# An mLSTM cell and a multiplicative feed-forward block in one kernel: output gate and weight exponential moved to ScalarE, units taken chunk by chunk, weight conversion spread over 18 units

## Chip, cores, metric

One NeuronCore of one Trainium2 chip. The metric is the device time of one execution in microseconds (us); medians of several runs. A run more than 1.5% above the fastest of its kernel counts as slow and is left out of the ratios. Engines in the profile: PE is TensorE (PEld its weight loads), DVE is VectorE, ACT is ScalarE, POOL is GpSimd, SP issues the transfers.

## The reference, cut to what matters

```python
# mLSTM cell: batch 4, heads 8, sequence 768, head dim 40; all float32
m_new  = max(f + m, i);  f_stab = exp(f + m - m_new);  i_stab = exp(i - m_new)
C = f_stab * C + i_stab * outer(v, k);   n = f_stab * n + i_stab * k
y = sigmoid(o) * (C @ q) / max(|n . q|, 1)
# then, on x = y as 3072 tokens x 320:
out = ((x @ w1) * (x @ w2)) @ w3 @ w_out     # d_ff 1024; the weights come as float64
```

## The kernel before

A **unit** is one chunk of 128 tokens of one batch with its 8 heads: 24 units. The loop has a **step** per unit. Its work on PE is: transposes of k and q (pt), scores (ss), state times q (pi), scores times v (ph), state update (pc), transposes of y (px). Four units make one group of 512 tokens for the feed-forward part: eight **ups** (128 columns of d_ff each: pa, pb) and four **downs** (128 tokens each: po). Before the downs, w3 and w_out have to be multiplied together, in eight **folds** (w3p, wp). The weights arrive as 64-bit words and are turned into float32 by seven DVE instructions per tile (34 **conversions**: 10 for w1 and w2, 8 for w_out, 16 for w3). In the views, pw is the tile of the weights that multiply the scores, h the cell's sum before the gate, y the result after it, st (later state) the state.

```python
def weights(n):                                     # b, c = divmod(n, NT): all chunks of a batch in turn
    nc.vector.tensor_tensor(out=pw, in0=pw, in1=aT[...], op=OP.add)              # pw [128, 8, 128]
    nc.gpsimd.affine_select(out=pw, in_=pw, ..., fill=-1.0e4, ...)
    nc.scalar.activation(out=pw, in_=pw, func=AF.Exp)
    nc.gpsimd.tensor_scalar(out=o, in0=o, scalar1=-87.0, scalar2=None, op0=OP.max)   # o [128, 320]
    nc.scalar.activation(out=o, in_=o, func=AF.Exp, scale=-1.0)
    nc.vector.tensor_scalar(out=o, in0=o, scalar1=1.0, scalar2=None, op0=OP.add)
    nc.vector.reciprocal(out=o, in_=o)
# ...
fold = {4: (0, 1), 5: (2,), 6: (3,), 7: (4, 5), 8: (6,), 9: (7,)}
for s in range(NU + LAG + 2 * GT):
    # ... loads for unit s + 2; weights(s); turn(s) (transposes)
    for _ in range(4):
        if w12_jobs:
            to_f32(*w12_jobs.pop(0))                # w1, w2: steps 0 to 2
    if 2 <= s < 4:
        for ko in range((s - 2) * FO // 2, (s - 1) * FO // 2):
            cvt_wo(ko)                              # w_out: steps 2, 3
    # ... first up; scores(s)
    for ko in fold.get(s, ()):
        cvt_w3(ko); w3_trans(ko); w3_mm(ko)         # w3: steps 4 to 9
    # ... cell(s - 1); second up; x_trans(s - 2); one down
```

## Time and profile before

| | before |
|---|---|
| median of 4 runs | 625.94 us (624.04 to 628.0) |
| span of the profiled run | 622.8 us |
| PE busy / DVE busy | 532.7 / 344.3 us |
| PE not busy | 622.8 - 532.7 = 90.1 us |

The prediction below shows the main views. One view is added here: what PE waited for in the first 300 us (engine, tile and line, released by; us in total, number of waits, the longest).

```profile
PE px L338 <- DVE h L289: 24.6, 2, 16.2
PE ss L273 <- DVE pw L276: 15.5, 2, 11.5
...
PE pi L287 <- DVE st L315: 11.8, 1, 11.8
PE wp L237 <- DVE w3T L231: 10.4, 5, 3.6
```

### The profile page before, as it was taken

How to read it: one execution, taken by the hardware profiler on the slowest of the kernel's cores; microseconds unless marked ns; L12 is line 12 of the kernel's file. 1: busy time of each engine (PE TensorE's matmuls, PEld its weight loads, DVE VectorE, ACT ScalarE, POOL GpSimd, SP SyncE). 2: the span in 40 equal slices, each digit the busy share in tenths (PEclk: the TensorE clock that was granted, in tenths of full speed). 3: DMA queues.
4: the chain of work that ended last, by engine and by line, in shares of the span. 5: the costliest groups of instructions: out<-in, count | busy, mean ns of one | idle time of the engine just before them, and what ended most of it. 6: DMA issues, size and time to landing. Idle time of an engine off the chain costs nothing.

```text
span 622.8 us, 6767 instructions
## 1 busy us (share of the span) xinstructions
PE 532.7 (86%) x2522; PEld 342.7 (55%) x2522; DVE 344.3 (55%) x648; ACT 118.9 (19%) x212; POOL 115.1 (18%) x129
## 2 busy tenths in 40 slices
PE   1362454588979899999999999999999999999997
PEld 1252353366646556665566665666665665554455
DVE  7499897988999844654464544644552332100000
ACT  2220011122122220222220222212221111111110
POOL 2261423323121121221121112211211000000000
PEclk9755555598999898999999999999999999999999
DMA  8698536446363132323334225334220000000001
GB/s 122 137 258 233 138 85 181 111 107 156 103 177 89 21 77 51 81 52 78 77 68 85 63 47 97 66 76 87 41 58 12 1 11 12 11 11 13 19 12 42
DMA packets 135488, 49.28 MB, mean 79 GB/s; under 512 B 103360, under 2 KB 131008, under 8 KB 135456
## 3 DMA queue, kind: packets, MB, share of 16 engines
q1 hardware_dynamic: 135456, 48.85, 33.8%
q8 instruction: 20, 0.33, 0.2%
q14 instruction: 12, 0.10, 0.1%
HBM read 44.81 MB, written 4.03 MB: 78 GB/s over the span
## 4 chain that ended last, share of the span: by engine, by line
PE 72%; DVE 17%; DMA 4%; SPq 2%; issue 2%; POOL 1%; ACT 0%; DVEq 0%; POOLq 0%; ACTq 0%
PE po L362 17%; PE pa L351 12%; PE pb L351 12%; PE pa L354 7%; PE wp L237 7%; PE ph L292 6%; PE pc L303 3%; PE pi L287 2%; PE ss L273 2%; PE pt L262 2%; DMA raw<-in_moe_w_dram 2%; DVE ex L138 2%; DVE mf L140 2%; DMA raw<-in_moe_w_out_dram 1%; SPq L107 1%
## 5 line engine op out<-in xcount | busy, mean ns | idle before, releaser
L357 DVE TENSOR_TENSOR ab<-pb,a_sb 128x512 f32<-128x512 f32 x48 | 33.0, 687 | 146.8 <-ACT a_sb L356 146.4
L362 PE MATMUL po<-w3o,ab 128*128 128x320 f32 x384 | 107.1, 434 | 0.0
L351 PE MATMUL pa<-xT,w 128*128 128x512 f32 x192 | 91.7, 600 | 0.0
L351 PE MATMUL pb<-xT,w 128*128 128x512 f32 x192 | 90.2, 592 | 0.0
L362 PEld LDWEIGHTS po<-w3o,ab 128*128 128x128 f32 x384 | 71.4, 190 | 30.3 <-issue 3.0
L356 ACT COPY a_sb<-pa 128x512 f32<-128x512 f32 x48 | 28.1, 584 | 237.6 <-PE pb L354 237.4
L351 PEld LDWEIGHTS pb<-xT,w 128*128 128x128 f32 x192 | 36.5, 190 | 45.9 <-issue 45.0
L246 DVE TENSOR_TENSOR pw<-pw,aT 128x1024 f32<-128x1024 f32 x24 | 29.8, 1242 | 45.1 <-DMA pw<-U_d 45.0
L292 PE MATMUL ph<-vbuf,pw 128*128 128x41 f32 x384 | 51.9, 298 | 3.1 <-ACT w3T L229 3.1
L354 PE MATMUL pa<-xT,wr 64*128 64x512 f32 x96 | 53.9, 641 | 0.0
L354 PE MATMUL pb<-xT,wr 64*128 64x512 f32 x96 | 53.9, 641 | 0.0
L292 PEld LDWEIGHTS ph<-vbuf,pw 128*128 128x128 f32 x384 | 50.7, 211 | 4.5 <-ACT w3T L229 3.4
L256 DVE RECIPROCAL o_in<-o_in 128x320 f32<-128x320 f32 x24 | 51.5, 2147 | 0.5
L237 PE MATMUL wp<-wo,w3T 128*128 128x320 f32 x128 | 42.8, 491 | 10.4 <-DVE w3T L231 10.4
L299 POOL TENSOR_TENSOR vw<-vbuf,wT 128x328 f32<-128x328 f32 x20 | 25.1, 1256 | 139.3 <-PE pc L303 123.4
L351 PEld LDWEIGHTS pa<-xT,w 128*128 128x128 f32 x192 | 33.2, 190 | 27.7 <-issue 26.7
L253 POOL TENSOR_SCALAR o_in<-o_in 128x320 f32<-128x320 f32 x24 | 36.5, 1519 | 60.9 <-DMA o_in<-in_o_gate_dram 60.9
L273 PE MATMUL ss<-qT,kT 64*128 64x128 f32 x384 | 31.8, 303 | 16.2 <-DVE pw L276 15.5
L273 PEld LDWEIGHTS ss<-qT,kT 64*128 64x128 f32 x384 | 30.2, 213 | 26.4 <-issue 13.2
L237 PEld LDWEIGHTS wp<-wo,w3T 128*128 128x128 f32 x128 | 26.7, 216 | 22.1 <-DVE w3T L231 11.6
L248 POOL TENSOR_SCALAR_AFFINE_SELECT pw<-pw 128x1024 f32<-128x1024 f32 x24 | 28.2, 1178 | 41.4 <-DVE pw L246 41.4
L338 PE MATMUL px<-ident,y 128*128 128x128 f32 x72 | 13.7, 302 | 24.6 <-DVE h L289 24.6
(77 smaller groups left out, 593.2 us busy)
## 6 DMA issues: line engine op xcount, KB each, us to landing
pw<-U_d SPq DMA_DIRECT2D x24, 512.0 KB, 5.3
raw<-in_moe_w_dram SPq DMA_DIRECT2D x24, 512.0 KB, 4.8
qbuf<-in_q_dram SPq DMA_DIRECT2D x24, 160.0 KB, 3.0
kbuf<-in_k_dram SPq DMA_DIRECT2D x24, 160.0 KB, 3.6
vbuf<-in_v_dram SPq DMA_DIRECT2D x24, 160.0 KB, 2.8
o_in<-in_o_gate_dram SPq DMA_DIRECT2D x24, 160.0 KB, 3.6
out_dram<-o_sb SPq DMA_DIRECT2D x24, 160.0 KB, 1.8
raw<-in_moe_w_out_dram SPq DMA_DIRECT2D x8, 320.0 KB, 3.3
```

Of the source, the lines that this page charges most:

```text
L237: nc.tensor.matmul(wp, lhsT=w3T[:, ki, :], rhs=wo[:, ki, :], start=(ki == 0), stop=(ki == FO - 1))
L246: nc.vector.tensor_tensor(out=pw, in0=pw, in1=aT[:, c, b * H:(b + 1) * H].unsqueeze(2).to_broadcast([L, H, L]), op=OP.add)
L248: nc.gpsimd.affine_select(out=pw, in_=pw, compare_op=OP.is_ge, fill=-1.0e4, base=0, pattern=[[0, H], [1, L]], channel_multiplier=-1)
L253: nc.gpsimd.tensor_scalar(out=o, in0=o, scalar1=-87.0, scalar2=None, op0=OP.max)
L256: nc.vector.reciprocal(out=o, in_=o)
L273: nc.tensor.matmul(ss[hip][:, p, :], lhsT=kT[r, p, :], rhs=qT[r, p, :], start=True, stop=True)
L292: nc.tensor.matmul(ph[:, hd, :], lhsT=pw[:, hd, :], rhs=vt[:, hd, :], start=True, stop=True)
L351: nc.tensor.matmul(p, lhsT=wt[:, cc, fs], rhs=x[:, cc, :], start=(cc == 0), stop=False)
L354: nc.tensor.matmul(p, lhsT=wr[r, fs], rhs=x[r, KF, :], start=False, stop=True)
L356: nc.scalar.copy(out=a_sb, in_=pa)
L357: nc.vector.tensor_tensor(out=ab_t[gr][:, f, :], in0=pb, in1=a_sb, op=OP.mult)
L362: nc.tensor.matmul(po, lhsT=ab_t[gr][:, f, j * L:(j + 1) * L], rhs=w3o[:, f, :], start=(f == 0), stop=(f == FO - 1))
```

## The change

Its intent: take work off DVE (the output gate becomes one Sigmoid on ScalarE for four units at once; the sum with `a` becomes the bias of the exponential), take the units chunk by chunk so that the state of a batch is needed only four units later, and hand out the conversions one to three a step, so that DVE's load fits beside the cell. A first stage for chunk 0 alone lets unit 0 start early.

```diff
-        nc.vector.tensor_tensor(out=pw, in0=pw, in1=aT[...], op=OP.add)
-        nc.gpsimd.affine_select(..., fill=-1.0e4, ...)
-        nc.scalar.activation(out=pw, in_=pw, func=AF.Exp)
+        for h in range(H):
+            nc.scalar.activation(out=pw[:, h, :], in_=pw[:, h, :], func=AF.Exp, bias=aT[:, c, b * H + h:...])
+        nc.gpsimd.affine_select(..., fill=0.0, ...)
-        # gate: max on GpSimd, exp on ScalarE, add and reciprocal on DVE, for each unit
+    def out_gate(c):
+        nc.scalar.activation(out=o_t[c], in_=o_t[c], func=AF.Sigmoid)      # [128, 4, 8, 40]
-        b, c = divmod(n, NT)
+        c, b = divmod(n, B)
-            st = sb.tile(...)                       # a new state tile for each unit
+        st = state[b]                               # one a batch, updated in place
-        nc.vector.tensor_scalar(out=den, in0=h[:, :, D:D1], scalar1=-1.0, scalar2=1.0, op0=OP.mult, op1=OP.max)
-        nc.vector.tensor_tensor(out=den, in0=h[:, :, D:D1], in1=den, op=OP.max)
+        nc.vector.tensor_scalar(out=den.bitcast(U32), ..., scalar1=0x7FFFFFFF, op0=OP.bitwise_and)
+        nc.vector.tensor_scalar(out=den, in0=den, scalar1=1.0, scalar2=None, op0=OP.max)
-    w1, w2: four a step from step 0; w_out: steps 2, 3; w3: steps 4 to 9
+    n_up = [0] * 6 + [2] * 8 + [0] * 6 + [2] * 6 + [4] * 5 + [0]
+    n_down = [0] * 18 + [2, 2, 1, 1, 1, 1, 2, 2, 0, 2, 2, 2, 2, 4]
+    cvt = {s: [("w12", 0, s)] for s in range(5)}
+    cvt.update({5: [w12 x3], 6: [w12 x2], 7: [wo x3], 8: [wo x3], 9: [wo x2]})          # shortened here
+    cvt.update({10 + ko: [("w3", ko)] for ko in range(8)})
```

Cut: the first stage for chunk 0, buffer counts (raw 3 to 2, xT 2 to 4), the mantissa of a conversion written in place.

More of the change, by code (lines that the diff above doesn't have):

```diff
@@ L54 @@
     REM = DM - KF * L
-    GT = 4
+    GT = B
     TG = GT * L
@@ L59 @@
     const = ctx.enter_context(tc.tile_pool(name="const", bufs=1))
-    gates = ctx.enter_context(tc.tile_pool(name="gates", bufs=1))
     wst = ctx.enter_context(tc.tile_pool(name="wst", bufs=2))
@@ L63 @@
     sb = ctx.enter_context(tc.tile_pool(name="sb", bufs=2))
-    ffn = ctx.enter_context(tc.tile_pool(name="ffn", bufs=2))
     dram = ctx.enter_context(tc.tile_pool(name="dram", bufs=1, space=bass.MemoryType.DRAM))
@@ L74, in mps @@
         return ps_m.tile(shape, FP, name=name, tag="m")
-    f_sb = gates.tile([BH, S], FP, name="f_sb")
-    a = gates.tile([BH, S], FP, name="a")
-    nc.sync.dma_start(out=f_sb, in_=f_gate.rearrange("b h s -> (b h) s"))
-    nc.sync.dma_start(out=a, in_=i_gate.rearrange("b h s -> (b h) s"))
     NB, NBQ = 4, 3
@@ L85 @@
     vbuf = [const.tile([L, H, D1], FP, name=f"vbuf{i}") for i in range(NB)]
-    for t in qbuf:
-        nc.gpsimd.memset(t[:, :, D:DP], 0.0)
-    for i in range(NB):
-        nc.gpsimd.memset(kbuf[i][:, :, D:DP], 0.0)
-        nc.gpsimd.memset(vbuf[i][:, :, D:D1], 1.0)
-    ident = const.tile([128, 128], FP, name="ident")
-    make_identity(nc, ident)
+    ident = const.tile([128, 128], FP, name="ident")
+    one = const.tile([BH, 1], FP, name="one")
+    state = [const.tile([128, NP, 2, D1], FP, name=f"state{b}") for b in range(B)]
@@ L95 @@
+    aT = const.tile([L, NT, BH], FP, name="aT")
+    gT = const.tile([L, NT, BH], FP, name="gT")
+    wT = const.tile([L, NT, BH], FP, name="wT")
+    decP = const.tile([128, B * NP, NT], FP, name="decP")
+    U_d = [dram.tile([BH, L], FP, name=f"U_d{c}") for c in range(NT)]
+    dec_d = dram.tile([BH, NT], FP, name="dec_d")
     o_t, u_t = {}, {}
     def load(n):
-        b, c = divmod(n, NT)
-        o_t[n] = io.tile([L, H, D], FP, name="o_in", tag="o_in", bufs=4)
-        for dst, src in ((qbuf[n % NBQ][:, :, 0:D], q), (kbuf[n % NB][:, :, 0:D], k),
-                         (vbuf[n % NB][:, :, 0:D], v), (o_t[n][:], o_gate)):
+        c, b = divmod(n, B)
+        for dst, src in ((qbuf[n % NBQ][:, :, 0:D], q), (kbuf[n % NB][:, :, 0:D], k), (vbuf[n % NB][:, :, 0:D], v)):
@@ L102, in load, with load_o @@
             nc.sync.dma_start(out=dst, in_=src[b, :, c * L:(c + 1) * L, :].rearrange("h p d -> p h d"))
+    def load_o(c):
+        o_t[c] = io.tile([L, B, H, D], FP, name="o_in", tag="o_in", bufs=2)
+        for b in range(B):
+            nc.sync.dma_start(out=o_t[c][:, b], in_=o_gate[b, :, c * L:(c + 1) * L, :].rearrange("h p d -> p h d"))
     def load_u(n):
-        b, c = divmod(n, NT)
+        c, b = divmod(n, B)
         u_t[n] = io.tile([L, H, L], FP, name="pw", tag="pw", bufs=4)
-        nc.sync.dma_start(out=u_t[n], in_=U_d[b * H:(b + 1) * H, c * L:(c + 1) * L]
-                          .unsqueeze(0).to_broadcast([L, H, L]))
@@ L110, with gate_cols @@
-    load(0)
-    load(1)
+        nc.sync.dma_start(out=u_t[n], in_=U_d[c][b * H:(b + 1) * H, :].unsqueeze(0).to_broadcast([L, H, L]))
+    with tc.tile_pool(name="gates", bufs=1) as gates:
+        f_sb = gates.tile([BH, S], FP, name="f_sb")
+        a = gates.tile([BH, S], FP, name="a")
+        nc.sync.dma_start(out=f_sb, in_=f_gate.rearrange("b h s -> (b h) s"))
+        nc.sync.dma_start(out=a, in_=i_gate.rearrange("b h s -> (b h) s"))
+        load(0)
+        nc.vector.memset(one, 1.0)
+        make_identity(nc, ident)
+        for i in range(NB):
+            nc.gpsimd.memset(kbuf[i][:, :, D:DP], 0.0)
+            if i < NBQ:
+                nc.gpsimd.memset(qbuf[i][:, :, D:DP], 0.0)
+            nc.gpsimd.memset(vbuf[i][:, :, D:D1], 1.0)
+        for t in state:
+            nc.gpsimd.memset(t, 0.0)
+        F = gates.tile([BH, S], FP, name="F")
+        U = gates.tile([BH, S], FP, name="U")
+        g, w = F, f_sb
+        m0 = gates.tile([BH, NT], FP, name="m0")
+        dec = gates.tile([BH, NT], FP, name="dec")
+        def gate_cols(src, dst, c0, c1):
+            pg = tps([L, c1 - c0, BH], "pg")
+            for c in range(c0, c1):
+                nc.tensor.transpose(pg[:, c - c0, :], src[:, c * L:(c + 1) * L], ident[0:BH, 0:BH])
+            nc.vector.tensor_copy(out=dst[:, c0:c1, :], in_=pg)
+        nc.vector.tensor_copy(out=f_sb[:, 0:1], in_=a[:, 0:1])
+        for c0, c1 in ((0, 1), (1, NT)):
+            rs = slice(c0 * L, c1 * L)
+            for c in range(c0, c1):
+                r = slice(c * L, (c + 1) * L)
+                nc.vector.tensor_tensor_scan(out=F[:, r], data0=one.to_broadcast([BH, L]), data1=f_sb[:, r], initial=0.0,
+                                             op0=OP.mult, op1=OP.add)
+                if c > 0:
+                    nc.vector.tensor_scalar(out=a[:, r], in0=a[:, r], scalar1=m0[:, c:c + 1], scalar2=None,
+                                            op0=OP.subtract)
+                nc.vector.tensor_tensor_scan(out=U[:, r], data0=f_sb[:, r], data1=a[:, r],
+                                             initial=0.0 if c else -1.0e30, op0=OP.add, op1=OP.max)
+                if c == 0:
+                    nc.vector.tensor_copy(out=m0[:, 1:2], in_=U[:, L - 1:L])
+                elif c < NT - 1:
+                    nc.vector.tensor_tensor(out=m0[:, c + 1:c + 2], in0=m0[:, c:c + 1],
+                                            in1=U[:, (c + 1) * L - 1:(c + 1) * L], op=OP.add)
+            nc.vector.tensor_tensor(out=U[:, rs], in0=F[:, rs], in1=U[:, rs], op=OP.subtract)
+            for c in range(c0, c1):
+                nc.sync.dma_start(out=U_d[c], in_=U[:, c * L:(c + 1) * L])
+            nc.vector.tensor_tensor(out=a[:, rs], in0=a[:, rs], in1=F[:, rs], op=OP.subtract)
+            gate_cols(a, aT, c0, c1)
+            if c0 == 0:
+                for n in range(2):
+                    load_u(n)
+                load_o(0)
+                load(1)
+            U3, w3d, a3 = (x.rearrange("p (c t) -> p c t", t=L)[:, c0:c1] for x in (U, w, a))
+            nc.vector.tensor_tensor(out=w3d, in0=a3, in1=U3[:, :, L - 1:L].to_broadcast([BH, c1 - c0, L]), op=OP.add)
+            nc.scalar.activation(out=dec[:, c0:c1], in_=U3[:, :, L - 1], func=AF.Exp)
+            nc.scalar.activation(out=g[:, rs], in_=U[:, rs], func=AF.Exp)
+            nc.scalar.activation(out=w[:, rs], in_=w[:, rs], func=AF.Exp)
+            gate_cols(w, wT, c0, c1)
+            if c0 > 0:
+                gate_cols(g, gT, c0, c1)
+        nc.sync.dma_start(out=dec_d, in_=dec)
+        for hip in range(2):
+            nc.sync.dma_start(out=decP[hip * DP:(hip + 1) * DP],
+                              in_=dec_d.rearrange("(n two) c -> two n c", two=2)[hip:hip + 1]
+                              .to_broadcast([DP, B * NP, NT]))
@@ L114 @@
+    ffn = ctx.enter_context(tc.tile_pool(name="ffn", bufs=2))
     wo = const.tile([128, FO, DM], FP, name="wo")
@@ L126, in to_f32 @@
         n = dst.shape[-1]
-        raw = wst.tile([128, n, 2], U32, name="raw", tag="raw", bufs=3)
+        raw = wst.tile([128, n, 2], U32, name="raw", tag="raw", bufs=2)
         for rows, src in pieces:
@@ L132, in to_f32 @@
         ma = wst.tile([128, n], U32, name="ma", tag="ma")
-        mf = wst.tile([128, n], FP, name="mf", tag="mf")
+        mf = ma.bitcast(FP)
         V = nc.vector
@@ L146, with cvt_w12 @@
     every = slice(0, 128)
-    w12_jobs = []
-    for c0 in range(0, DFF, CW):
-        for dst, src in ((w1, w1_d), (w2, w2_d)):
-            for ko in range(KF):
-                w12_jobs.append((dst[:, ko, c0:c0 + CW], [(every, src[ko * 128:(ko + 1) * 128, cols(c0, CW)])]))
-        w12_jobs.append((wr[:, c0:c0 + CW], [(slice(j * REM, (j + 1) * REM), src[KF * L:DM, cols(c0, CW)])
-                                             for j, src in enumerate((w1_d, w2_d))]))
+    def cvt_w12(half, i):
+        c0 = half * CW
+        if i < 2 * KF:
+            dst, src = ((w1, w1_d), (w2, w2_d))[i // KF]
+            ko = i % KF
+            to_f32(dst[:, ko, c0:c0 + CW], [(every, src[ko * 128:(ko + 1) * 128, cols(c0, CW)])])
+        else:
+            to_f32(wr[:, c0:c0 + CW], [(slice(j * REM, (j + 1) * REM), src[KF * L:DM, cols(c0, CW)])
+                                       for j, src in enumerate((w1_d, w2_d))])
     def cvt_wo(ko):
@@ L161, in cvt_w3 @@
             to_f32(w3_t[ko][:, c0:c0 + CW], [(every, w3_d[ko * 128:(ko + 1) * 128, cols(c0, CW)])])
-    one = const.tile([BH, 1], FP, name="one")
-    nc.vector.memset(one, 1.0)
-    F = gates.tile([BH, S], FP, name="F")
-    U = gates.tile([BH, S], FP, name="U")
-    g, w = F, f_sb
-    m0 = gates.tile([BH, NT], FP, name="m0")
-    dec = gates.tile([BH, NT], FP, name="dec")
-    nc.vector.tensor_copy(out=f_sb[:, 0:1], in_=a[:, 0:1])
-    for c in range(NT):
-        r = slice(c * L, (c + 1) * L)
-        nc.vector.tensor_tensor_scan(out=F[:, r], data0=one.to_broadcast([BH, L]), data1=f_sb[:, r], initial=0.0,
-                                     op0=OP.mult, op1=OP.add)
-        if c > 0:
-            nc.vector.tensor_scalar(out=a[:, r], in0=a[:, r], scalar1=m0[:, c:c + 1], scalar2=None, op0=OP.subtract)
-        nc.vector.tensor_tensor_scan(out=U[:, r], data0=f_sb[:, r], data1=a[:, r], initial=0.0 if c else -1.0e30,
-                                     op0=OP.add, op1=OP.max)
-        if c == 0:
-            nc.vector.tensor_copy(out=m0[:, 1:2], in_=U[:, L - 1:L])
-        elif c < NT - 1:
-            nc.vector.tensor_tensor(out=m0[:, c + 1:c + 2], in0=m0[:, c:c + 1], in1=U[:, (c + 1) * L - 1:(c + 1) * L],
-                                    op=OP.add)
@@ L187 @@
-    nc.vector.tensor_tensor(out=U, in0=F, in1=U, op=OP.subtract)
-    U_d = dram.tile([BH, S], FP, name="U_d")
-    nc.sync.dma_start(out=U_d, in_=U)
-    nc.vector.tensor_tensor(out=a, in0=a, in1=F, op=OP.subtract)
-    U3 = U.rearrange("p (c t) -> p c t", t=L)
-    nc.vector.tensor_tensor(out=w.rearrange("p (c t) -> p c t", t=L), in0=a.rearrange("p (c t) -> p c t", t=L),
-                            in1=U3[:, :, L - 1:L].to_broadcast([BH, NT, L]), op=OP.add)
-    nc.scalar.activation(out=dec, in_=U3[:, :, L - 1], func=AF.Exp)
@@ L195 @@
-    nc.scalar.activation(out=g, in_=U, func=AF.Exp)
-    nc.scalar.activation(out=w, in_=w, func=AF.Exp)
-    aT = const.tile([L, NT, BH], FP, name="aT")
-    gT = const.tile([L, NT, BH], FP, name="gT")
-    wT = const.tile([L, NT, BH], FP, name="wT")
-    decP = const.tile([128, B * NP, NT], FP, name="decP")
-    dec_d = dram.tile([BH, NT], FP, name="dec_d")
-    nc.sync.dma_start(out=dec_d, in_=dec)
-    for hip in range(2):
-        nc.sync.dma_start(out=decP[hip * DP:(hip + 1) * DP],
-                          in_=dec_d.rearrange("(n two) c -> two n c", two=2)[hip:hip + 1]
-                          .to_broadcast([DP, B * NP, NT]))
@@ L210, in gate_cols @@
-    def gate_cols(src, dst):
-        pg = tps([L, NT, BH], "pg")
-        for c in range(NT):
-            nc.tensor.transpose(pg[:, c, :], src[:, c * L:(c + 1) * L], ident[0:BH, 0:BH])
-        nc.vector.tensor_copy(out=dst, in_=pg)
     w3T_t = {}
@@ L238, in w3_mm @@
         nc.scalar.copy(out=w3o[:, ko, :], in_=wp)
-    qT_t, kT_t, c_t, y_t, x_t, s_t, e_t = {}, {}, {}, {}, {}, {}, {}
+    qT_t, kT_t, y_t, x_t = {}, {}, {}, {}
+    def out_gate(c):
+        nc.scalar.activation(out=o_t[c], in_=o_t[c], func=AF.Sigmoid)
     def weights(n):
-        b, c = divmod(n, NT)
+        c, b = divmod(n, B)
         pw = u_t[n]
-        nc.vector.tensor_tensor(out=pw, in0=pw, in1=aT[:, c, b * H:(b + 1) * H].unsqueeze(2).to_broadcast([L, H, L]),
-                                op=OP.add)
-        nc.gpsimd.affine_select(out=pw, in_=pw, compare_op=OP.is_ge, fill=-1.0e4, base=0,
+        for h in range(H):
+            nc.scalar.activation(out=pw[:, h, :], in_=pw[:, h, :], func=AF.Exp, bias=aT[:, c, b * H + h:b * H + h + 1])
+        nc.gpsimd.affine_select(out=pw, in_=pw, compare_op=OP.is_ge, fill=0.0, base=0,
                                 pattern=[[0, H], [1, L]], channel_multiplier=-1)
-        nc.scalar.activation(out=pw, in_=pw, func=AF.Exp)
-        o = e_t[n] = o_t.pop(n)
-        nc.gpsimd.tensor_scalar(out=o, in0=o, scalar1=-87.0, scalar2=None, op0=OP.max)
-        nc.scalar.activation(out=o, in_=o, func=AF.Exp, scale=-1.0)
-        nc.vector.tensor_scalar(out=o, in0=o, scalar1=1.0, scalar2=None, op0=OP.add)
-        nc.vector.reciprocal(out=o, in_=o)
     def turn(n):
@@ L278, in cell @@
     def cell(n):
-        b, c = divmod(n, NT)
+        c, b = divmod(n, B)
         pw, vt = u_t.pop(n), vbuf[n % NB]
         qT = qT_t.pop(n)
+        st = state[b]
         hs = slice(b * H, (b + 1) * H)
@@ L287, in cell @@
                 nc.tensor.matmul(pi[:, 2 * p:2 * p + 2, :].rearrange("p a b -> p (a b)"), lhsT=qT[:, p, :],
-                                 rhs=c_t[n - 1][:, p].rearrange("p a b -> p (a b)"), start=True, stop=True)
+                                 rhs=st[:, p].rearrange("p a b -> p (a b)"), start=True, stop=True)
             nc.vector.tensor_tensor(out=h, in0=pi, in1=gT[:, c, hs].unsqueeze(2).to_broadcast([L, H, D1]), op=OP.mult)
@@ L305, in cell @@
                                  rhs=vw[:, 2 * p:2 * p + 2, :].rearrange("p a b -> p (a b)"), start=True, stop=True)
-            st = sb.tile([128, NP, 2, D1], FP, name="st", tag="st")
-            if c == 0:
-                nc.gpsimd.memset(st, 0.0)
-            else:
+            if c > 0:
                 nc.gpsimd.tensor_tensor(
-                    out=st.rearrange("p n a b -> p n (a b)"), in0=c_t[n - 1].rearrange("p n a b -> p n (a b)"),
+                    out=st.rearrange("p n a b -> p n (a b)"), in0=st.rearrange("p n a b -> p n (a b)"),
                     in1=decP[:, b * NP:(b + 1) * NP, c:c + 1].to_broadcast([128, NP, 2 * D1]), op=OP.mult)
@@ L315, in cell @@
                 nc.vector.tensor_tensor(out=st[r, :, hip, :], in0=pc[r, :, hip, :], in1=st[r, :, hip, :], op=OP.add)
-            c_t[n] = st
-        c_t.pop(n - 1, None)
         den = sb.tile([L, H, 1], FP, name="den", tag="den")
-        nc.vector.tensor_scalar(out=den, in0=h[:, :, D:D1], scalar1=-1.0, scalar2=1.0, op0=OP.mult, op1=OP.max)
-        nc.vector.tensor_tensor(out=den, in0=h[:, :, D:D1], in1=den, op=OP.max)
+        nc.vector.tensor_scalar(out=den.bitcast(U32), in0=h[:, :, D:D1].bitcast(U32), scalar1=0x7FFFFFFF, scalar2=None,
+                                op0=OP.bitwise_and)
+        nc.vector.tensor_scalar(out=den, in0=den, scalar1=1.0, scalar2=None, op0=OP.max)
         nc.vector.reciprocal(out=den, in_=den)
-        e = e_t.pop(n)
+        e = o_t[c][:, b]
         nc.vector.tensor_tensor(out=e, in0=e, in1=den.to_broadcast([L, H, D]), op=OP.mult)
@@ L333, in x_trans @@
         if j == 0:
-            x_t[gr] = ffn.tile([128, KF + 1, TG], FP, name="xT", tag="xT")
+            x_t[gr] = ffn.tile([128, KF + 1, TG], FP, name="xT", tag="xT", bufs=4)
         y = y_t.pop(n)
@@ L365, in ffn_out @@
         nc.scalar.copy(out=o_sb, in_=po)
-        t0 = (gr * GT + j) * L
+        t0 = j * S + gr * L
         nc.sync.dma_start(out=out[t0:t0 + L, :], in_=o_sb)
-    for n in range(3):
-        load_u(n)
-    gate_cols(a, aT)
-    gate_cols(g, gT)
-    gate_cols(w, wT)
-    LAG = 2
-    UPS = FO // GT
-    up = [(gr, f) for gr in range(NG) for f in range(FO)]
-    down = [(gr, j) for gr in range(NG) for j in range(GT)]
-    fold = {4: (0, 1), 5: (2,), 6: (3,), 7: (4, 5), 8: (6,), 9: (7,)}
-    for s in range(NU + LAG + 2 * GT):
-        u = s - LAG - GT
-        ups = up[u * UPS:(u + 1) * UPS] if u >= 0 else []
-        downs = down[u - GT:u - GT + 1] if u >= GT else []
+    LAG = 2
+    ups = [(gr, f) for gr in range(NG) for f in range(FO)]
+    downs = [(gr, j) for gr in range(NG) for j in range(GT)]
+    n_up = [0] * 6 + [2] * 8 + [0] * 6 + [2] * 6 + [4] * 5 + [0]
+    n_down = [0] * 18 + [2, 2, 1, 1, 1, 1, 2, 2, 0, 2, 2, 2, 2, 4]
+    cvt = {s: [("w12", 0, s)] for s in range(5)}
+    cvt.update({5: [("w12", 1, 0), ("w12", 1, 1), ("w12", 1, 2)], 6: [("w12", 1, 3), ("w12", 1, 4)]})
+    cvt.update({7: [("wo", i) for i in range(3)], 8: [("wo", i) for i in range(3, 6)], 9: [("wo", i) for i in range(6, 8)]})
+    cvt.update({10 + ko: [("w3", ko)] for ko in range(8)})
+    out_gate(0)
+    for s in range(max(len(n_up), len(n_down))):
         if s + 2 < NU:
             load(s + 2)
-        if 0 < s and s + 2 < NU:
             load_u(s + 2)
+            if s % B == 1 and s // B + 1 < NT:
+                load_o(s // B + 1)
         if s < NU:
@@ L392 @@
             turn(s)
-        for _ in range(4):
-            if w12_jobs:
-                to_f32(*w12_jobs.pop(0))
-        if 2 <= s < 4:
-            for ko in range((s - 2) * FO // 2, (s - 1) * FO // 2):
-                cvt_wo(ko)
-        if ups:
-            ffn_up(*ups[0])
+        now = [ups.pop(0) for _ in range(n_up[s] if s < len(n_up) else 0)]
+        for x in now[:1]:
+            ffn_up(*x)
         if s < NU:
             scores(s)
-        for ko in fold.get(s, ()):
-            cvt_w3(ko)
-            w3_trans(ko)
-            w3_mm(ko)
+        for job in cvt.get(s, ()):
+            kind, args = job[0], job[1:]
+            if kind == "w12":
+                cvt_w12(*args)
+            elif kind == "wo":
+                cvt_wo(*args)
+            else:
+                cvt_w3(*args)
+                w3_trans(*args)
+                w3_mm(*args)
         if 0 <= s - 1 < NU:
             cell(s - 1)
-        for x in ups[1:]:
+        if s % B == 3 and s // B + 1 < NT:
+            out_gate(s // B + 1)
+        for x in now[1:]:
             ffn_up(*x)
@@ L412 @@
             x_trans(s - LAG)
-        for x in downs:
-            ffn_out(*x)
+        for _ in range(n_down[s] if s < len(n_down) else 0):
+            ffn_out(*downs.pop(0))
+    assert not ups and not downs
 _INS = ['q', 'k', 'v', 'i_gate', 'f_gate', 'o_gate', 'moe_w1', 'moe_w2', 'moe_w3', 'moe_w_out']
```

## The prediction

> **What bounds the kernel now.** I read the page's utilisation slices first, then busy time by windows, then the groups of instructions, then the chain that ended last.
>
> ```profile
> PE 532.7 (86%) x2522; PEld 342.7 (55%) x2522; DVE 344.3 (55%) x648; ACT 118.9 (19%) x212; POOL 115.1 (18%) x129
> ...
> PE   1362454588979899999999999999999999999997
> ...
> DVE  7499897988999844654464544644552332100000
> ...
> PEclk9755555598999898999999999999999999999999
> ```
>
> A slice is 15.6 us. Up to about slice 16 (250 us) DVE is at 8 or 9 tenths and PE is not full, at half clock for a long stretch. After it PE is full at full clock and DVE at 4 to 6 tenths. So there are two stages with two bounds: DVE first, PE after. The windows say it in us (busy by PE, PEld, DVE, ACT, POOL, then clock, DMA share, GB/s):
>
> ```profile
> 50.00:100.00 50.00, 18.70 (x91) 17.76 (x91) 44.12 (x109) 3.64 (x6) 12.36 (x9) 0.50 0.53 135
> 150.00:200.00 50.00, 45.33 (x231) 29.66 (x229) 45.83 (x92) 12.06 (x21) 10.75 (x10) 1.00 0.50 130
> 300.00:350.00 50.00, 50.00 (x238) 30.30 (x238) 24.72 (x35) 12.69 (x23) 11.17 (x13) 1.00 0.34 73
> ```
>
> In the chain, the distance between two rows gives the PE time of a piece of work at full clock:
>
> ```profile
> 350.95 1.05 PE pi L287 x8
> ...
> 370.26 1.05 PE pi L287 x8
> ...
> 574.67 1.72 PE pa L351 x4
> 576.39 1.72 PE pb L351 x4
> 579.17 1.91 PE pa L351 x4
> ...
> 583.86 4.50 PE po L362 x16
> ```
>
> A full steady unit is 370.26 - 350.95 = 19.3 us: two ups (one 128-column block of the feed-forward part for 512 tokens), one down (the output of 128 tokens) and one cell. An up is 579.17 - 574.67 = 4.5 us, or 583.86 - 579.17 = 4.7; a down is 4.3 to 4.5. The cell is left with 19.3 - 2 x 4.5 - 4.3 = 6.0. A fold of w3 is 16 wp matmuls of 0.27 us plus 8 transposes, about 5.3. All PE work warm: 24 x 6.0 + 48 x 4.55 + 24 x 4.35 + 8 x 5.3 = 509 us. The span is 623, so about 110 us are lost, nearly all before 250 us. That is what a change can win.
>
> **What the Trainium skill says.** (1) "ScalarE: Activation LUTs", section "What ACT_TABLE_LOAD costs": an ACTIVATE with immediate bias takes 186 ns + 0.833 ns per element, with a per-partition pointer bias about 280 ns + 0.833, and neighbours overlap by about 93 ns. The trace agrees for the immediate form: the 128x1024 exponential takes 1058 ns against 1039 worked out. The pointer form is not in this trace. (2) Same page, "Table sets: the hidden batching unit": exp and sigmoid are in different sets, so each switch is a load; the one load in the trace took 1283 ns, as stated there. (3) "TensorE: Matmul & The Clock Gate", Part 1: the clock is halved unless PE has been busy for a window of about 3.4 us. The trace shows 0.50 from about 25 to 120 us, and also that "busy" as the profile counts it is not enough:
>
> ```profile
> 85.00:90.00 5.00, 5.00 (x29) 4.70 (x31) 4.94 (x9) 2.67 (x4) 2.99 (x2) 0.50 0.19 33
> 90.00:95.00 5.00, 5.00 (x29) 4.78 (x25) 5.00 (x17) 0.04 (x1) 0.27 (x1) 0.50 0.20 34
> 120.00:125.00 5.00, 5.00 (x20) 3.60 (x19) 4.82 (x11) 0.59 (x1) 0.00 (x0) 0.83 0.47 152
> ```
>
> Ten us of cell matmuls left it at 0.50; the first burst of wide wp matmuls raised it.
>
> **The change part by part.** The groups that go:
>
> ```profile
> L256 DVE RECIPROCAL o_in<-o_in 128x320 f32<-128x320 f32 x24 | 51.5, 2147 | 0.5
> L246 DVE TENSOR_TENSOR pw<-pw,aT 128x1024 f32<-128x1024 f32 x24 | 29.8, 1242 | 45.1 <-DMA pw<-U_d 45.0
> L253 POOL TENSOR_SCALAR o_in<-o_in 128x320 f32<-128x320 f32 x24 | 36.5, 1519 | 60.9 <-DMA o_in<-in_o_gate_dram 60.9
> L250 ACT ACTIVATE pw<-pw 128x1024 f32<-128x1024 f32 x24 | 25.4, 1058 | 34.8 <-POOL pw L248 34.8
> L255 DVE TENSOR_SCALAR o_in<-o_in 128x320 f32<-128x320 f32 x24 | 12.6, 523 | 13.9 <-ACT o_in L254 13.9
> ```
>
> *DVE* loses 51.5 + 29.8 + 12.6 = 93.9 us, and about 6 more on the denominator (a tensor_tensor of 443 ns becomes a tensor_scalar of about 171). 344 becomes about 244: 4.5 us per unit for the cell (two mults of 0.68, two h operations of 0.49, two state updates of 0.33, 0.55 of denominator, 0.98 for e and y), 3.5 us per 512-wide conversion (seven rows of 0.39 to 0.73), about 2.35 per 320-wide one.
>
> *ACT* gives 25.4 + 11.2 and takes 24 x 8 biased exponentials of 128: (280 + 107 - 93) = 294 ns each by the page, 2.4 us a unit, 58 in all; six sigmoids of 1280 columns (1.25 each) and 12 more table loads (the built order shows 13 in all), 15 us. ACT goes from 119 to about 163 of some 590: a helper still, and at 6 us in a 15 to 20 us step not on the path. The exception is the start, where the built order puts the first sigmoid, which waits for its load, ahead of the copy of qT for unit 0.
>
> *POOL* loses 36.5 us, all off the path. *DMA bytes* are the same, some weights move later. *State*: a batch's next chunk is now four units away, so pi no longer waits for the state just written (11.8 us once in the waits).
>
> *The order* is where most of the time lies. Ups start at step 6 as before, but a step before that carries one conversion, not four; w3 is folded at steps 10 to 17 with ups beside steps 10 to 13; steps 14 to 17 hold cell and fold only. I take each stretch as the larger of PE and DVE, plus a margin for in-order waits (in 150 to 200 us both engines stood at 91%):
>
> - Start to step 6: gates of chunk 0 only; u, o and q, k, v of two units (2.8 MB) at some 190 GB/s, so the first scores at about 18 us. PE then sits at half clock (no wide matmul before step 6): cold rows are ss 2.4, ph 3.6, pc 2.0, pt 2.1, px 0.9, so 11 us for units 0 to 3, which have no pi, and 13 for units 4 and 5. DVE needs 4.5 + 3.5 = 8.0, then 15 at step 5 with three conversions. 18 + 4 x 11 + 13 + 15 = 90, less some 6 for overlap: 84.
> - Steps 6 to 9: PE 6 + 9 = 15, DVE about 13: 16.5 x 4 = 66.
> - Steps 10 to 13: PE 6 + 9 + 5.3 = 20.3, DVE 13.6: 21 x 4 = 84.
> - Steps 14 to 17: PE 11.3, DVE 4.5 + 7.0 + 0.7 = 12.2: 13.5 x 4 = 54.
> - Steps 18, 19: PE 6 + 2 x 4.3 = 14.6: 30 for both.
> - Steps 20 to 23: the steady 19.3: 77.5.
> - Rest, PE alone: last cell 3.5, 24 ups of 4.65 = 111.5, 16 downs of 4.4 = 70.5, last copy and store 3.5 (as 619.3 to 622.8 now): 189.
>
> The sum is 584.5. The timed median stands 2 us over the profiled span now, so 586 us: 6 to 7% faster. Of the 100 us taken from DVE only some 39 come back, because after 250 us DVE was not the bound.
>
> **Rivals.** (a) *PE stays warm in steps 0 to 5.* Then a step is set by DVE's 8 us, or by the DMA's 1.5 MB at 190 to 250 GB/s (6 to 8 us), so about 9, and step 6 starts near 75: 577 us. Against it stand the two rows at 0.50 with full PE. (b) *The loads become the bound of the start.* A step needs 480 KB of 160-byte rows, 512 KB of U and 512 KB of weights; slice 0 shows a DMA share of 8 tenths at 122 GB/s. If they take 13 us a step, step 6 starts near 100: 602. (c) *The in-order DVE holds PSUM buffers*: conversions of 3.5 us lie between the scores and ab operations, and three buffers serve pa, pb and po. Steps 6 to 17 then cost DVE plus waits, some 2 us more each: 610. (d) *ScalarE's new waits*: exponentials and table loads ahead of kT, qT and a_sb. At 6 us of 15 this should cost below 5 us in all: 590. (e) *Little gain*, since the second stage is PE-bound: it would need the early loss to stay at 110 us although DVE loses 4 us in each unit. I see nothing for it.
>
> **Range and chances.** (a) gives 577 and (c) 610; early conversions going better than the margins would give 565. I take 565 to 606. Two rivals together would be needed to come within 2% (612 or more): 0.04. Slower by 2%: 0.01. Faster: 0.95.
>
> **What would show it.** Right: DVE busy about 245, ACT about 160, POOL about 78; first pa matmul at about 84 us; clock 0.50 until then, 1.0 after; PE full from about step 18 (290 us) to the end; the stretch from the last unit's scores to the end near 189 us. Wrong: clock 1.0 in steps 0 to 5 (rival a), DMA share near 1 with DVE waiting for raw or pw before 100 us (b), PE idle behind DVE ab or w3T in steps 6 to 17 (c), PE behind ACT kT, qT or pw (d). The prediction fails as a whole if PE is below 90% busy between 150 and 300 us.

## The result, and the profile after

The changed kernel takes 575.69 us (575.07 to 576.82, 4 runs); ratio 0.9204, 95% interval 0.917 to 0.9238. A ratio here is the mean time of one kernel's fast runs over that of the other's of the same rounds, so not quite the ratio of the medians quoted. The prediction was 586, range 565 to 606.

The page of the changed kernel (busy by engine, then 40 slices of 14.3 us):

```profile
PE 532.6 (93%) x2521; PEld 339.2 (59%) x2521; DVE 256.7 (45%) x581; ACT 166.2 (29%) x377; POOL 72.6 (13%) x105
...
PE   0869899889698999999999999999999999999997
...
DVE  7356989997978665765431332132001101010100
...
PEclk9985799989798998999999999999999999999999
```

PE is busy 532.6 us, as before (532.7). So the whole gain is PE idle time: 573.4 - 532.6 = 40.8 us not busy, against 90.1. The gain in span is 49.4 us, the gain in idle time 49.3. The DVE row no longer falls from 8 tenths to 4 at once (before: at slice 14, 218 us): it falls step by step, and PE stands mostly at 8 or 9 tenths from the second slice.

PE's waits in the first 300 us are now short:

```profile
PE pg L134 <- DVE a L158: 11.5, 2, 6.0
PE wp L257 <- DVE w3T L251: 5.5, 2, 3.3
PE pt L278 <- DMA kbuf<-in_k_dram: 4.6, 2, 3.7
PE px L351 <- DVE h L306: 3.5, 2, 1.9
```

The first is the start itself (gates before any work). The wait of px for h went from 24.6 to 3.5 us, those of ss for pw and of pi for the state are gone from the list.

The groups that were added or changed (busy us, mean ns, idle before and its releaser):

```profile
L270 ACT ACTIVATE pw<-pw,aT 128x128 f32<-128x128 f32 x192 | 60.1, 391 | 24.7 <-DMA pw<-U_d 24.6
...
L208 DVE SCALAR_TENSOR_TENSOR ex<-raw,ex 128x512 uint32<-128x512 uint32 (+1 forms) x34 | 24.6, 722 | 0.1
...
L264 ACT ACT_TABLE_LOAD x6 | 7.7, 1283 | 8.4 <-DMA o_in<-in_o_gate_dram 8.4
L270 ACT ACT_TABLE_LOAD x6 | 7.7, 1283 | 10.4 <-DMA pw<-U_d 10.3
```

### The profile page after: what moved, and what is told of

Read it like the earlier page. It is cut to its first block, busy times and chain, and to the rows that moved or that the text cites. A ratio compares the mean times of both kernels' runs of the same rounds, so it can differ in the third digit from the quotient of the medians.

```text
span 573.4 us, 6858 instructions
## 1 busy us (share of the span) xinstructions
PE 532.6 (93%) x2521; PEld 339.2 (59%) x2521; DVE 256.7 (45%) x581; ACT 166.2 (29%) x377; POOL 72.6 (13%) x105
## 4 chain that ended last, share of the span: by engine, by line
PE 78%; DVE 13%; DMA 4%; ACT 2%; SPq 1%; issue 1%; ACTq 0%; DVEq 0%
PE po L375 18%; PE pa L364 12%; PE pb L364 12%; PE pa L367 7%; PE wp L257 7%; PE ph L309 6%; PE pt L278 4%; PE ss L289 4%; PE pc L320 3%; PE pi L304 3%; DMA kbuf<-in_k_dram 2%; DMA raw<-in_moe_w_dram 2%; DVE pw L292 2%; DVE ex L208 2%; PE px L351 1%; DVE ma L210 1%
## 5 line engine op out<-in xcount | busy, mean ns | idle before, releaser
L364 PE MATMUL pa<-xT,w 128*128 128x512 f32 x192 | 93.9, 610 | 0.5 <-ACT xT L352 0.5
L270 ACT ACTIVATE pw<-pw,aT 128x128 f32<-128x128 f32 x192 | 60.1, 391 | 24.7 <-DMA pw<-U_d 24.6
L309 PEld LDWEIGHTS ph<-vbuf,pw 128*128 128x128 f32 x384 | 48.8, 203 | 3.7 <-DVE pw L292 1.3
L257 PE MATMUL wp<-wo,w3T 128*128 128x320 f32 x128 | 40.8, 475 | 5.6 <-DVE w3T L251 5.5
L271 POOL TENSOR_SCALAR_AFFINE_SELECT pw<-pw 128x1024 f32<-128x1024 f32 x24 | 31.6, 1316 | 104.4 <-ACT pw L270 103.6
L292 DVE TENSOR_TENSOR pw<-ss,pw 128x512 f32<-128x512 f32 x48 | 30.9, 682 | 11.2 <-PE ss L289 11.1
L367 PEld LDWEIGHTS pa<-xT,wr 64*128 64x128 f32 x96 | 14.1, 184 | 36.5 <-issue 35.5
L289 PEld LDWEIGHTS ss<-qT,kT 64*128 64x128 f32 x384 | 28.2, 210 | 10.1 <-issue 6.2
L378 ACT COPY o_sb<-po 128x320 f32<-128x320 f32 x24 | 10.2, 425 | 78.3 <-PE po L375 75.5
L320 PE MATMUL pc<-vw,kbuf 128*128 128x82 f32 x160 | 24.6, 302 | 0.1
```

Of the source, the lines that this page charges most:

```text
L257: nc.tensor.matmul(wp, lhsT=w3T[:, ki, :], rhs=wo[:, ki, :], start=(ki == 0), stop=(ki == FO - 1))
L270: nc.scalar.activation(out=pw[:, h, :], in_=pw[:, h, :], func=AF.Exp, bias=aT[:, c, b * H + h:b * H + h + 1])
L271: nc.gpsimd.affine_select(out=pw, in_=pw, compare_op=OP.is_ge, fill=0.0, base=0, pattern=[[0, H], [1, L]], channel_multiplier=-1)
L289: nc.tensor.matmul(ss[hip][:, p, :], lhsT=kT[r, p, :], rhs=qT[r, p, :], start=True, stop=True)
L292: nc.vector.tensor_tensor(out=pv[:, :, hip, :], in0=ss[hip], in1=pv[:, :, hip, :], op=OP.mult)
L309: nc.tensor.matmul(ph[:, hd, :], lhsT=pw[:, hd, :], rhs=vt[:, hd, :], start=True, stop=True)
```

## The experiments

Three theories of the gain. **Theory 1:** it is the DVE work removed (the two ScalarE parts). **Theory 2:** it is the order of units, with its longer distance between states, and the early start. **Theory 3:** it is the timetable of the conversions. All kernels below gave a correct result but one.

### Each part undone in the changed kernel

**Old output gate (e1).**

```diff
-        nc.scalar.activation(out=o_t[c], in_=o_t[c], func=AF.Sigmoid)
+        # in weights(n), o = o_t[c][:, b]: max on GpSimd, exp on ScalarE, add 1 and reciprocal on DVE
```

> The changed kernel with the old output gate alone: clamp on GpSimd, exp on ScalarE, add and reciprocal on DVE, a batch at a time; no Sigmoid, so one table load. Theory 1 (the gain is DVE work taken from the stage in which DVE was the bound): DVE busy rises by 24 x 2.67 = 64 us to about 320; 2.67 us a unit counts in full in steps 6 to 13, mostly in 14 to 17, little in 0 to 5 and after 18: 575.7 becomes about 608 (600 to 616). Theory 2 (the gain is the order of units and the early start): under +10 us. Theory 3 (the gain is the spread of the conversions): under +10 us.

Measured: 594.66 us, ratio to before 0.9499 (0.9442 to 0.9555): +19 us, DVE busy 309.5. More than theories 2 and 3 allow, less than theory 1 expected. (The profiled run was the fastest, 587.8; the other three were at 594 to 596.)

**Old sum with a (e2).**

```diff
-        for h in range(H): nc.scalar.activation(..., func=AF.Exp, bias=aT[...]);  affine_select(fill=0.0)
+        nc.vector.tensor_tensor(out=pw, in0=pw, in1=aT[...], op=OP.add);  affine_select(fill=-1.0e4)
+        nc.scalar.activation(out=pw, in_=pw, func=AF.Exp)
```

> The changed kernel with the old sum on DVE and one 1024-wide exponential after the select, in place of eight biased ones. Theory 1: 1.24 us a unit more on DVE, so about 10 us in steps 6 to 13 and 4 in 14 to 17: 590 (585 to 595). Theories 2 and 3: under +5 us; it could even gain, since ScalarE is relieved of 34 us.

Measured: 581.26 us, ratio 0.9316 (0.9277 to 0.9355): +5.6 us. The sign is theory 1's, the size a third to a half of it.

**Old timetable of the conversions (e3).**

```diff
-    cvt: w12 steps 0 to 6, wo 7 to 9, w3 10 to 17
+    cvt: w12 four a step from step 0, wo steps 2 and 3, w3 {4: (0, 1), 5: (2,), 6: (3,), 7: (4, 5), 8: (6,), 9: (7,)}
```

> The changed kernel with the old timetable of conversions (four a step from step 0, w3 folded in steps 4 to 9); ups and downs stay where they are. Theory 3: PE starves behind DVE in steps 0 to 9 and cannot use the slack later: +15 to +25 us (590 to 600). Theory 1: DVE has the same sum to do before it stops being the bound; steps 0 to 9 end near 190 us in place of 139, but steps 10 to 17 then are PE-bound at 15 and 6 us a step, 85 in place of 142: within 8 us of 575.7.

Measured: 613.87 us, ratio 0.9833 (0.9803 to 0.9862): +38 us, more than even theory 3 expected. With the same instructions on every engine, the timetable alone takes back three quarters of the gain. PE in order of time (start, us, instruction, count; idle before it and its releaser):

```profile
65.88 2.08 PE L289 MATMUL ss<-qT,kT 64*128 64x128 f32 x16 [1.00 <-ACT qT L281]
105.52 1.08 PE L246 MATMUL w3p<-ident,w 128*128 128x128 f32 x4 [37.56 <-DVE w L211]
```

Between the scores of unit 4 and the first w3 transpose PE does nothing for 37.6 us. In that time DVE is never idle for more than about 1 us at a stretch and runs conversions of w1, w2, w_out and w3. The cell's next matmuls come after w3's in PE's own order: ph of unit 3 runs at 120.9 us, though DVE had written its pw by 54.3 us. My working for theory 1 was wrong in method: I compared the two engines' sums over ten steps (190 us), where the larger of the two has to be taken step by step. By steps, DVE is busy 98.8 of the 123.9 us before step 5, with PE at 54.6; in steps 5 to 9, with up to two folds in a step, PE is busy 102.2 of 108.5 us, and step 10 began at 232 us.

**Old order of units (e4).**

```diff
-        c, b = divmod(n, B)
+        b, c = divmod(n, NT)      # gate input of four consecutive units together; U of unit 1 loaded after chunk 1's gates
```

> The changed kernel with the units in the old order (all chunks of a batch in turn); output gate still four units at a time. Unit 1 now needs chunk 1's gates, and each pi the state of the unit just before. Theory 2: the state chain stalls PE while DVE is loaded with conversions, +12 us or more (588 or more). Theory 1 and 3: later start and five more cold pi, about +3 to +5 us (579 to 581).

Measured: 576.56 us over four runs; two of them (579.9 and 581.9) count as slow, the two fast ones give ratio 0.9154 (0.9119 to 0.919). The profile fell on a slow run. Nothing is lost by the old order, so this part of theory 2 falls. The state of the unit just before is nearly always ready: in e13 below, which has the old order too and whose profile is of a fast run, pi waits for it once, 3.1 us. The early start stays in e4, so this run does not test it.

### Parts alone

**The two ScalarE parts alone, on the kernel before (e5).**

```diff
-        # DVE sum and one exponential; max, exp, add, reciprocal for the gate
+        # eight biased exponentials; one Sigmoid for four units (loaded together); mantissa in place, for room
```

> The kernel before with only the two ScalarE parts: Sigmoid gate of four units at once and biased exponential; its order of units, its first stage and its timetable of conversions stay (the conversion also writes its mantissa in place to make room). Theory 1: 93.9 us off DVE, 3.9 us a unit over some 11 units of the DVE stage: 625 becomes 585 (578 to 592). Theories 2 and 3: 610 or more.

Measured: 612.16 us, ratio 0.9814 (0.9771 to 0.9856): 12 us. DVE busy falls to 255.6 us, as in the changed kernel, and the time hardly moves. PE's waits in this kernel:

```profile
PE ss L276 <- DVE pw L279: 31.3, 3, 14.0
PE px L341 <- DVE h L292: 20.0, 2, 15.5
```

The long waits for DVE remain. Theory 1 alone falls.

This run also bears on theory 2. e3 has the same two ScalarE parts and the old times of the conversions, but the new order, the early start and the new times of ups and downs as well; at 613.87 us (ratio 0.9833) it is no faster than e5, though unit 2 starts its transposes at 30.8 us in e3 and at 41.2 in e5. So with the old times of the conversions these other parts gain nothing. No run undoes the early start or the times of ups and downs alone in the changed kernel.

**The new order and timetable alone (e10):** both old DVE parts back, e1 and e2 together.

```diff
-        # out_gate: Sigmoid; weights: eight biased exponentials
+        # gate by max, exp, add, reciprocal (as e1); DVE sum and one exponential (as e2)
```

> The changed kernel with both old ScalarE-side parts back (old gate and old sum): the new order and timetable alone. Old gate alone cost 19 us and old sum alone 5.6 in the earlier runs. If the parts add, 600 (597 to 604). If the two together push DVE back over PE in the steps where one alone left slack (steps 14 to 17, and 0 to 5), more than the sum: 605 to 615. DVE busy about 340.

Measured: 603.66 us, ratio 0.9668 (0.9617 to 0.9719), DVE busy 336.9: inside the range for parts that add. Of the 29.1 us of span over the changed kernel, 17.8 are PE idle time and 11.3 PE busy time, for the same matmuls (543.9 us against 532.6, at a mean granted clock of 0.935 against 0.958). This is the fourth corner of a square (its lower row also has the early start, the times of ups and downs, the shorter denominator and the buffer counts of the changed kernel):

| ratio to before | old ScalarE parts | new ScalarE parts |
|---|---|---|
| old timetable and order | 1 | 0.9814 (e5) |
| new timetable and order | 0.9668 (e10) | 0.9204 |

Alone they give 1.9 and 3.3%, in sum 5.2; together 8.0. Some 2.8% (17 us; by the intervals, give or take 0.8%) come only when both are there. A reading that no run tests by itself: spreading makes room between the conversions for the cell's DVE instructions; the shorter the cell's own DVE work, the better it fits there. In e10 PE still has one such wait, before step 6:

```profile
74.42 1.98 PE L326 MATMUL pc<-vw,kbuf 128*128 128x82 f32 x8
87.68 0.90 PE L357 MATMUL px<-ident,y 128*128 128x128 f32 x3 [11.28 <-DVE h L312]
```

**Which part of the timetable (e11):** w1, w2 and w_out early again, w3 late.

```diff
-    cvt: w12 steps 0 to 6, wo 7 to 9, w3 10 to 17
+    cvt: w12 steps 0 to 2, wo steps 2 and 3, w3 10 to 17
```

> The changed kernel with w1, w2 and w_out on the old timetable (steps 0 to 3), w3 late as in the changed kernel (steps 10 to 17). Early conversion of everything cost 38 us. Working by steps: DVE has 14 + 35 + 19 + 4 x 4.5 = 86 us to do before step 4, so step 6 starts near 105 in place of 72; steps 6 to 13 then are PE-bound (15.2 and 20.5), 143 us in place of 163: 575.7 + 33 - 20 = 589 (584 to 594). If only the lead of w3 had done the harm: 578 or less.

Measured: 583.86 us, ratio 0.9334 (0.9288 to 0.938): +8 us, just under the range of the first expectation. So about 8 of e3's 38 us belong to w1, w2 and w_out, about 30 to the lead of w3. The delay is there (first pa at 99.3 us in place of 72.5), and two thirds of it are won back by step 18: 4 us in steps 6 to 9 (63.2 us in place of 67.5) and 12 in steps 10 to 13 (84.0 in place of 96.0). DVE had then converted 4 of the 16 pieces of w3 before step 10, so that 8 fell in steps 10 to 13, where the changed kernel has 12.

### Smaller questions

**Tables (e6):** gate by tanh, which the exponential's table set holds too.

```diff
-        nc.scalar.activation(out=o_t[c], in_=o_t[c], func=AF.Sigmoid)
+        nc.scalar.activation(out=o_t[c], in_=o_t[c], func=AF.Tanh, scale=0.5)    # e = (tanh + 1) * den, den = 1 / max(2|nq|, 2)
```

> The changed kernel with the gate as (1 + tanh(o/2)) / 2, one half folded into the denominator: if tanh needs no table of its own beside exp, ScalarE loses 12 table loads (15.4 us). Theory: ScalarE is off the path, so under 4 us gained (572 to 576). Rival (ScalarE's in-order waits at the start are on the path): 6 us or more gained.

Measured: 574.56 us, ratio 0.9209 (0.9149 to 0.9268): no change, with one table load left:

```profile
L167 ACT ACT_TABLE_LOAD x1 | 1.3, 1283 | 0.8 <-PEq L443 0.8
```

ScalarE lost 15.7 us of busy time (166.2 to 150.5) for nothing: it is off the path.

**Order of the first loads (e7):** gate input of chunk 0 after q, k and v of three units, its sigmoid after the first scores.

> The changed kernel with the gate input of chunk 0 loaded after q, k, v of units 0 to 2 and its sigmoid put after the first scores. Theory: the start is bound by loads, and the PE wait for k that ends with the clock halved at about 40 us goes; first pa moves from 72.5 to about 64: 568 (564 to 571). Rival: the same bytes have to come, DVE and PE wait elsewhere: 574 to 577.

Measured: 576.09 us, ratio 0.9232 (0.9205 to 0.926): the rival held. Unit 2's transposes start at 24.8 us in place of 29.4, but then y waits for its gate:

```profile
PE px L350 <- DVE y L339: 4.9, 1, 4.9
PE ss L288 <- ACT qT L280: 3.8, 1, 3.8
```

and the first pa comes at 72.3 us, as before.

**A third raw buffer (e8).**

```diff
-        raw = wst.tile([128, n, 2], U32, name="raw", tag="raw", bufs=2)
-        ma = wst.tile([128, n], U32, name="ma", tag="ma")
+        raw = wst.tile([128, n, 2], U32, name="raw", tag="raw", bufs=3)
+        ma = wst.tile([128, n], U32, name="ma", tag="ma", bufs=1)               # for room
```

> The changed kernel with three raw buffers in place of two (ma down to one for room). Theory: conversions in steps 5 to 12 wait for raw (9.4 us of DVE waits, with one of 6.8 us at 137 us on the chain): 6 to 10 us gained (566 to 570). Rival: the loads are spread by the order of issue, not by buffers: within 3 us.

Measured: 573.16 us, ratio 0.9183 (0.9136 to 0.923): within the noise of the changed kernel.

**Are the loads the bound of the start? (e12)** The DMA share is 1.0 or more from 40 to 70 us.

```diff
+        if 4 <= n <= 6:
+            return                # in load(n): no q, k, v for units 4 to 6
```

> Wrong result on purpose: the changed kernel without the loads of q, k and v of units 4, 5 and 6 (they compute on what the buffers hold), 1.44 MB less before step 6. If the loads bound steps 2 to 6 (DMA share about 1.0 from 40 to 70 us): at some 210 GB/s, 7 us less, first pa at about 65 in place of 72.5. If the half clock of PE or DVE's order bounds them: first pa at 71 to 73.

Measured: one run, 570.64 us; the first pa came at 76.5 us, which neither expectation had. Step 5 began 3.9 us earlier than in the changed kernel (56.0 us in place of 59.9), but step 6 4 us later. So fewer loads did not bring the first pa forward. The time from 60 to 80 us, first in the changed kernel, then here (busy PE, PEld, DVE, ACT, POOL, clock, DMA share, GB/s):

```profile
60.00:80.00 20.00, 17.09 (x100) 12.68 (x99) 18.32 (x37) 8.83 (x25) 4.99 (x7) 0.83 1.00 191
```

```profile
60.00:80.00 20.00, 15.77 (x64) 12.81 (x65) 19.91 (x40) 7.60 (x23) 5.70 (x6) 0.57 0.85 193
```

Two things hold step 6 up. PE waits longer within step 5 (2.2 us for kT, 2.7 for y, with DVE busy 19.9 of 20 us), and the clock is at 0.50 from 61.9 to 79.0 us, where the changed kernel is back at 1.00 at 63.4. So the run does not separate the loads from the clock. Step 10 begins at 140.4 us in place of 139.1, and step 18 at 276.8 in place of 281.3. One run; the 5 us are not more than the spread of e8.

**Three small parts together (e13).**

```diff
+        # e4: b, c = divmod(n, NT);  e6: gate by tanh;  e8: raw bufs=3, ma bufs=1
```

> Batch-major units, tanh gate and three raw buffers together on the changed kernel: each alone was within noise or up to 3 us better. If they add: 567 (563 to 571). If they are noise: 572 to 577.

Measured: 570.64 us (565.93 to 572.19, 6 runs), ratio 0.911 (0.9066 to 0.9153), about 1% under the changed kernel's 0.9204. It is the fastest kernel; which of the three parts carries the 1% is not settled.

### Where the differences lie

Start of some steps in us (first transpose of k of that unit on PE), and the rest to the end of the profiled span:

| | first pa | step 10 | step 18 | span | span - step 18 |
|---|---|---|---|---|---|
| changed kernel | 72.5 | 139.1 | 281.3 | 573.4 | 292.1 |
| e1 old gate | 74.5 | 146.0 | 295.0 | 586.1 | 291.1 |
| e2 old sum | 74.2 | 143.7 | 284.7 | 577.8 | 293.1 |
| e3 old timetable | 138.5 | 232.4 | 322.5 | 611.6 | 289.1 |
| e10 new order and timetable alone | 90.5 | 155.1 | 311.0 | 602.5 | 291.5 |
| e11 w3 late only | 99.3 | 160.5 | 290.9 | 583.1 | 292.2 |
| e12 no loads | 76.5 | 140.4 | 276.8 | 568.9 | 292.1 |

The last column is the same within 4 us: from step 18 on the kernel is PE's (busy 288.7 of 292.1 us in the changed kernel), and every difference is made before it. A late first pa costs less than its delay when the steps after it are PE-bound (e11), and an early unit before it won nothing (unit 2 in e7, unit 5 in e12): by step 6 the lead was gone.

## Why the prediction was right, point by point

**Two stages, DVE first, PE after; some 110 us lost, nearly all before 250 us.** Right, but DVE's row falls to 4 tenths at 218 us, not at 250. The gain of 49 us is PE idle time, and the stage after step 18 keeps its length in every kernel with the new times of ups and downs.

**The order and the timetable are where most of the time lies.** Right in the outcome, but the text gave no split between the parts; e3, e5 and e10 give it: 1.9% for the ScalarE parts alone, 3.3% for the rest alone, 2.8% for the two together. Within the rest it is the timetable; the order of units gives nothing that e4 can show, and the wait of pi for the state, named as a gain of "11.8 us once", was not the order's to give.

**DVE 244 us.** 256.7. The removed rows went as worked out, the denominator too. The conversion rows grew by about 9 us in total: the row at L208 takes 722 ns in the mean where the same row took 632 before:

```profile
L138 DVE SCALAR_TENSOR_TENSOR ex<-raw,ex 128x512 uint32<-128x512 uint32 (+1 forms) x34 | 21.5, 632 | 0.0
```

The two traces say where the growth lies. In each kernel 67 of the 238 conversion instructions overlap a GpSimd instruction in time. The other 171 exceed the median of their row by at most 15 ns; the 67 together take 3.5 us more than that in the kernel before and 11.7 in the changed one (L208 at 512 wide: 863 ns in the mean beside GpSimd, 678 without). Why the overlap costs more in the changed kernel is not settled.

**ScalarE 163 us, off the path.** 166.2, of which the biased exponentials are 60.1 (58 worked out), the 12 added loads 12 x 1.283 = 15.4. The pointer form that "ScalarE: Activation LUTs" of the Trainium skill gives in "What ACT_TABLE_LOAD costs" fits: 280 + 0.833 x 128 = 387 ns, measured 391. In a run of eight only seven overlap, so an estimate from that page is (8 x 387 - 7 x 93) / 8 = 306 ns each, not the 294 of the prediction; measured 60.1 us / 192 = 313. e6 shows the loads off the path. **GpSimd 78 us:** 72.6.

**The stretches.** In us, from the starts of the steps:

| steps | predicted | measured |
|---|---|---|
| start to 6 | 84 | 71.6 |
| 6 to 9 | 66 | 67.5 |
| 10 to 13 | 84 | 96.0 |
| 14 to 17 | 54 | 46.2 |
| 18, 19 | 30 | 29.4 |
| 20 to 23, and rest | 266.5 | 262.7 |

The start was mis-sized by 12 us, and the term is the first three steps. From the scores of unit 0 to those of unit 3, 3 x 11 = 33 us were worked out; they took 21.2 (20.7 to 41.9 us). The rest partly cancels: the first scores came 2.7 us later than the 18 worked out, and from the scores of unit 3 to step 6 it took 29.7 us, not 33. The assumption behind the 11 us, half clock until the first wide matmul, failed:

```profile
45.00:50.00 5.00, 5.00 (x25) 5.00 (x25) 1.09 (x3) 0.00 (x0) 0.71 (x2) 0.50 1.11 204
...
60.00:65.00 5.00, 5.00 (x33) 4.54 (x32) 4.64 (x11) 3.99 (x11) 1.01 (x2) 0.66 1.07 211
65.00:70.00 5.00, 2.93 (x25) 2.75 (x24) 5.00 (x10) 0.40 (x1) 2.15 (x2) 1.00 1.39 162
```

The clock was at 1.00 from 29.3 to 39.5 us, where unit 2 ran its transposes and scores in the full-clock times (scores 1.16 us, against 1.98 for unit 0), at 0.50 from 39.5 to 63.4, at 1.00 to 70.3, and at 0.50 once more to 73.7, over the first pa at 72.5. How much of the 12 us is the clock's was not tested. Of the stretches 10 to 13 and 14 to 17, the sum was right (138 predicted, 142 measured), the division was not:

```profile
139.10:235.10 96.00, 86.78 (x431) 55.73 (x430) 70.19 (x153) 31.90 (x74) 14.99 (x18) 0.93 0.49 134
235.10:281.30 46.20, 45.57 (x335) 38.38 (x334) 26.52 (x60) 19.73 (x47) 9.19 (x14) 1.00 0.44 96
```

In steps 14 to 17 DVE is busy 26.5 us, 6.6 a step, where I had 12.2: the built order lets DVE run ahead with conversions of later steps (12 of the 16 pieces of w3 in steps 10 to 13, not 8), so that these four steps are PE's alone at 11.6 us (11.3 worked out), while PE loses 9 us of idle time in steps 10 to 13, most of it waiting for w3T (5.5) and w3 (2.3). In e11, with 8 pieces there, steps 10 to 13 take the 84 us predicted.

That the total came within 2% is partly luck: the stretches were predicted 12 us too long at the start and 12 too short in steps 10 to 13, which cancels.

**The rivals.** (a) half true: full clock for a part of the start. (b) not borne out: the DMA share was 1.0 or more, but in e12, a single run, fewer loads brought nothing by step 6, with the clock against it. (c) is the nearest to what remains: PE waits for w3T, h and w3 in steps 6 to 17, but some 11 us, not 24. (d) small: e6 takes the table loads away and wins nothing, and PE's waits for ScalarE's copies kT, qT, xT and w3T sum to 3.8 us in the first 300. (e) did not come.

## What to carry to other kernels

Busy sums over a stage are not a bound when an engine runs its instructions in the order built, as PE did in e3: take the larger engine step by step, and look for the one long wait in which the other engine stands behind a run of work that is not urgent. A helper's bulk work is best handed out in pieces as small as the gaps, beside the steps in which the main engine has enough of its own; here that was worth more than removing 94 us from the helper, and the removal only paid in full once the work was spread. Before tuning loads or tables, ask whether the stage's end moves at all: the starts of a few steps in a table show it in one look.

## What the Trainium skill lacked or had wrong

- "TensorE: Matmul & The Clock Gate", Part 1, gives a window of about 3.4 us of activity for the full clock. It does not say what counts as activity: from 45 to 60 us the profile shows PE busy for 14.6 of 15 us (5.00, 4.58 and 5.00), with small cell matmuls, at a clock of 0.50; at 63.4 us it rose, with the same kind of work and before any wide matmul. What tripped it is open.
- The same page says that clock events in a trace have been seen to be unreliable. Here they agree with the matmuls at the places checked: 16 score matmuls took 2.00 us at 27.5 us (0.50 from 25.9 to 29.3) and 1.16 us at 32.3 us (1.00). What misleads is the time before the first event, at 22.5 us: the views print 1.00 for it, while 16 score matmuls took 1.98 us at 20.7 us, against 1.06 us at full clock (93.6 us). The page does not say how to read that time.
